# mLSTM attention and a squared-ReLU FFN on one core: from chunk 10 on, an even chunk's attention goes directly behind the FFN1 section, and FFN2 runs unbroken

## The chip, the cores and the metric

The kernel runs on one core of one Trainium2 chip. Times are device microseconds of that core. The engines are named as in the profile: PE (TensorE matmuls), PEld (its weight loads), DVE (VectorE), ACT (ScalarE), POOL (GpSimd), SP (SyncE, which here only issues DMAs). L405 means line 405 of the kernel.

## What is computed

Four batches of eight heads with 768 tokens and a head size of 40 go through an mLSTM cell; its output, reshaped to 3072 rows of 320, goes through an FFN with a squared ReLU and 2048 hidden columns. Inputs and output are float32.

```python
# attention, for each token t (C, n and m are the running state of a head)
m_new = maximum(f[t] + m, i[t])
f_stab, i_stab = exp(f[t] + m - m_new), exp(i[t] - m_new)
C = f_stab * C + i_stab * outer(v[t], k[t])
n = f_stab * n + i_stab * k[t]
y[t] = sigmoid(o[t]) * (C @ q[t]) / maximum(abs(n @ q[t]), 1.0)
# FFN on x = y, reshaped to (3072, 320)
h = maximum(x @ w_in, 0)
out = (h * h) @ w_out
```

## The kernel before

**Chunks.** The attention is done in 24 chunks of 128 tokens, six to a batch. Chunk s is computed in chunk form: scores of keys against queries (`scores`, L565), a weight for each pair from the gates (`weigh`, L498: eight exponentials on ACT, then `vw` on POOL), their product (`weighted`, two operations on DVE, L608), and `attend_begin` and `attend_end` (L774, L835), which multiply these with the values, add the part of the carried state C, and make the next state. The first chunk of a batch (0, 6, 12, 18) has no part of C (L799); the last makes no new state.

**FFN.** Two chunks make a group of 256 rows. FFN1 of a group is done in two halves, each `ffn1_open` (four accumulators X, Y, V, Z in four PSUM banks), then `ffn1_close`, and `ffn1_rows` (L1165), 64 records in which 64x64 pieces of the array are used for the last 64 rows of w_in. The closing ends in one ACT operation and four DVE adds (L1181 to L1185). FFN2 is `ffn2_fast`, four steps of 32 PE records (L1056). Both are a Strassen-like scheme with seven products, so each step is followed by adds, and sums of operands (`sums`, L1051) are made on DVE. Full-array matmuls (FFN1's main part, FFN2) and 64-row ones (scores, attention, rows) alternate on PE.

**The order.** Everything is issued in an order written out by hand, and each engine works in that order. From chunk 6 on, the loop at L1426 goes through parts n, four to a section: section s = 6 + n // 4, and `at` = n % 4. An even section is FFN2 of a group, an odd one FFN1 of a group two further; the last sections, from 24 on, have no attention. In each section of chunk s stand:

- even s, at 0: `scores(s)`, the transpose of the next chunk's keys and queries (`turn_kq`, L403 to L405, DVE), `weighted(s)`, then FFN2's first step, then `ffn1_square` for the second half of the FFN1 section before it (four ACT operations)
- even s, at 1: `attend_begin(s)`, `scores(s + 1)`, `attend_end(s)`, then the second FFN2 step
- odd s, at 1 (between FFN1's first opening and closing): `attend_begin(s)`, `ffn1_rows`, `attend_end(s)`; behind the closing `turn_kq(s + 1)`
- at 1 also, behind `attend_end`: `decays(s + 1)` (ACT, L496), `mask(s + 1)` (POOL, L478), `decay_C(s + 1)` (POOL, Cd), loads of later chunks (POOL's DMAs), and on SP `store_num` (L868, the transposed result tn to DRAM), `load_num` (L873, four DMAs), `load_squares(s + 2)` (L398, four DMAs: keys and queries of chunk s + 2 into one of the two kqT buffers), and in even sections `load_A(s + 2)` (L429, two DMAs)
- at 2: FFN's third step or second opening; then `weigh(s + 1)`, in even sections `weighted(s + 1)`, `normalise_turned(s)` (ten DVE operations, L885 to L898), `store_rows` and `load_rows` (SP); in odd sections `load_A(s + 2)`; `scale_q(s + 1)` (DVE, L761)
- at 3: FFN's last step or second closing, and DMA issues of POOL for later chunks

**The write that separates the two halves of attention.** The last thing of `attend_begin` is a one-element DVE operation. It reads an element that the half's last matmuls write, and writes into a spare column of the keys, which the first weight load of `attend_end` reads:

```python
# L787, L790
end, spare = out[1][DP : DP + 1, 2 * P + D1 : 2 * P + D1 + 1], d["kq"][DP : DP + 1, 0, 2, DP - 1 :]
nc.vector.tensor_scalar(spare, end, scalar1=0.0, scalar2=None, op0=ALU.mult)
```

So PE enters `attend_end` only when DVE has come to this operation in its own order.

**PSUM.** In this loop three banks (`at`) hold the attention's two outputs and some scores, and five (`h_ps`) are used in turn by FFN1, FFN2 and the scores that ask for "h".

Of the kernel before, what the change touches and what calls it, by code (L numbers as in the profile page):

```python
# [29 lines left out]
def kernel(  # L30
# [372 lines left out]
    def turn_kq(s):  # L403
        t = kqT_b[s % NKT][:].rearrange("p n j t -> p (n j t)")
        nc.vector.transpose(t, t)  # L405
# [159 lines left out]
    def scores(s, o=(False, False)):  # L565
        d = st[s]

        sc = [bank(o[i]) for i in range(2)]
        d["sc"] = sc
        if s >= KQ_SQ:  # L570
            if s >= ROT:
                d["sc"] = [t.rearrange("p j t -> p (j t)")[:, : 3 * P].rearrange("p (e t) -> p e t", e=2) for t in sc]
            for e in range(2):
                for late_keys in range(2):
                    for c in range(2):
                        for i in range(2):
                            rows = slice(DP * i, DP * i + D)
                            start = e == late_keys == 0
                            if s < ROT:
                                j, keys = 2 * late_keys + e, HALVES[c]  # L580
                                to, t0 = sc[i][HALVES[c], j, :], 0
                            else:
                                j, keys = 2 * (c ^ late_keys) + e, HALVES[late_keys]
                                to = d["sc"][i][HALVES[c], e, slice(0, DP) if late_keys else slice(DP, 3 * DP)]
                                t0 = DP * late_keys
                            nc.tensor.matmul(  # L586
                                to, lhsT=d["kT"][rows, j, keys], rhs=d["qT"][rows, j, t0:], start=start, stop=True,
                                skip_group_check=True,
                            )
            return  # L590
        for j in range(PR):
            for i in range(2):
                rows = slice(DP * i, DP * i + D)
                nc.tensor.matmul(  # L594
                    sc[i][:, j, :], lhsT=d["kT"][rows, j, :], rhs=d["qT"][rows, j, :], start=True, stop=True,
                )
# [556 lines left out]
    def ffn1_rows(g, q, first):  # L1153
        xT, xs = st["xT", g], st["xs"]
        X, Y, V, Z = st["f1"]
        lo, hi = HALVES
        pairs = (
            ((X, lo, xT[lo, 0, 2, :], False), (Y, hi, xT[hi, 1, 2, :], first)),
            ((V, lo, xT[lo, 1, 2, :], first), (Z, hi, xs[hi, 1, :], False)),
        )  # L1160
        for pair in pairs:
            for n in range(4):
                for cols in HALVES:
                    for to, rows, rhs, start in pair:
                        nc.tensor.matmul(  # L1165
                            to[cols, n, :], lhsT=w_in2[rows, 4 * q + n, cols], rhs=rhs,
                            start=(start and n == 0), stop=True, skip_group_check=True,
                        )
# [34 lines left out]
    def do(f, s):  # L1203
        if 0 <= s < NT:
            f(s)
# [97 lines left out]
    for u in range(8):  # L1303
        s = 2 + u // 2
# [114 lines left out]
    for g in range(NG):  # L1419
        parts += [(2, g, i) for i in range(4)]  # L1420
        if g + 2 < NG:
            parts += [(1, g + 2, i) for i in range(4)]
    ROUNDED = (17, 18)
    assert ROUNDED[-1] == len(pieces)

    for n, (which, g, i) in enumerate(parts):  # L1426
        s, at = NB + n // 4, n % 4
        if n == len(ROUNDED):
            brought.close()
            late = ctx.enter_context(tc.tile_pool(name="late", bufs=1, side="right"))  # L1430
        even = s % 2 == 0
        fast = which == 1
        if n == 2:
            half_tanh(6)
            half_tanh(7)
        if at == 0 and even:
            do(scores, s)
            if n > 0:
                do(turn_kq, s + 1)
            do(weighted, s)  # L1440
        if n == 0:
            turn_kq(7)
            pair_up(8)
            load_rows(4)
            rounding.words()
            rounding.join()
        if at == 1:
            do(attend_begin, s)
            if n == 5:
                sums_of_weights(3)  # L1450
            if even:
                do(lambda s: scores(s, ("h", "h")), s + 1)
            if fast:
                ffn1_rows(g, 0, True)
            do(attend_end, s)
            do(decays, s + 1)
            do(mask, s + 1)
            if not even and not fast:
                do(turn_kq, s + 1)
            do(decay_C, s + 1)  # L1460
            if not fast and not even:
                do(turn_squares, s - 1)
            if even and s > NB:
                do(load, s + 3)
            do(store_num, s)
            if n == 1:
                normalise_turned(5)
                store_rows(5)
                turn_squares(4)
            if n == 5:  # L1470
                load_rows(6)
            do(load_num, s)
            if n == 1:
                load_rows(5)
                weigh(7, masked=True)
                sums_of_win(2)
            do(load_squares, s + 2)
            if even:
                do(load_A, s + 2)
        if n == 3:  # L1480
            load_o(8)
            load_o(9)
            sums_of_weights(0)
        if n == 8:
            sums(1, slice(0, NPAIR), (3,))
        if n == 9:
            sums(1, slice(0, NPAIR), (4,))
            sums_of_weights(2)
            turn_squares(6)
        if which == 2 and i == 3 and g == NG - 2:  # L1490
            sums(g + 1, slice(0, NPAIR), (2,))
        if which == 2 and g > 1 and i < 2:
            sums(g, slice(0, NPAIR), (3 + i,))
        if at == 3 and even and NB < s and s // 2 - 1 < NG:
            sums_of_x(s // 2 - 1)
        if at == 2 and not fast:
            if even and n > 2:
                do(turn_squares, s - 1)
            do(scale_q, s + 1)
        if at == 3:  # L1500
            if s % 4 == 3:
                for r in range(s + 1, min(s + 5, NT) if n > 7 else 10):
                    half_tanh(r)
        if n == 10:
            half_tanh(10)
            half_tanh(11)
        if fast:
            if i % 2:
                if n == 7:
                    sums(1, slice(0, NPAIR), (2,))  # L1510
                ffn1_close(g, i // 2, i == 1)
                if at == 1:
                    do(turn_kq, s + 1)
                    if n > 5:
                        do(turn_squares, s - 1)
            else:
                ffn1_open(g, i // 2)
                if i == 0 and g > 2:
                    sums(g - 1, slice(0, NPAIR), (2,))
            if at == 2:  # L1520
                do(scale_q, s + 1)
            if n == 6:
                sums(1, slice(0, NPAIR), (1,))
        elif g == 0:
            ffn2(i)
        else:
            ffn2_fast(g, i)
        if at == 2:
            if n > 2:
                do(lambda s: weigh(s, masked=True), s + 1)  # L1530
            ffn1_square()
            if even:
                do(weighted, s + 1)
            do(normalise_turned, s)
            do(store_rows, s)
            if n == 2:
                pair_up(9)
                turn_squares(5)
                sums_of_x(2)
                load(8)  # L1540
            if not even:
                do(load_A, s + 2)
            if n > 2:
                do(load_o, s + 5)
                do(load_rows, s)
            if s == NB + 1:
                pair_up(s + 3)
        if n in (5, 6):
            load(4 + n)
            load_o(5 + n)  # L1550
        if even and at == 3 and s > NB:
            do(pair_up, s + 3)
            do(pair_up, s + 4)
        if even and at == 3 and s > NB:
            do(load, s + 4)
        if n == 4:
            sums_of_weights(1)
        if n == 3:
            turn_halves()
        if n in (12, 25):  # L1560
            spread_slots(2 + n // 25)
        if at == 0:
            ffn1_square()
        if n < len(ROUNDED):
            while rounding.done < ROUNDED[n]:
                rounding.step()
# [30 lines left out]
```

## Time and profile before

| what | us |
|---|---|
| median of three runs | 487.77 |
| the three runs | 487.77, 488.3, 483.75 |
| span of the profiled execution | 484.7 |
| PE busy in it | 476.5 |
| DVE busy in it | 342.4 |
| one FFN2 section from chunk 10 on, first score matmul to next FFN1 | 18.3 to 19.3 |

The profile gives its span, from the first to the last instruction, and no separate time for that execution; one of the three runs is 1.0 below this span and two are 3.0 and 3.6 above it, so what lies around the span can't be told from the scatter between executions. A line of a timeline gives the start in us, the time taken, the engine, the line of the kernel, the operation with its output and inputs, the tile and the number of merged records; a bracket behind it gives the idle time of the engine and what ended it. Matmuls overlap, so starts, not durations, are what costs are read from.

### The profile page before, as it was taken

Reading aid. Unit: us, or ns where it says so; the run is one execution under the profiler, and the core shown is the slowest. Engines: PE = TensorE matmul, PEld = TensorE weight load, DVE = VectorE, ACT = ScalarE, POOL = GpSimd, SP = SyncE. Lnnn points to the kernel's source line nnn. Section 1 sums busy time; section 2 is a strip of 40 time slices with the busy share of each in tenths; the row PEclk is TensorE's granted clock in tenths of the full one; section 3 lists DMA queues with packets and bytes.
Section 4 is the critical chain, followed back from the end, with each engine's and each line's share of the span. In section 5 each row is a group of like instructions: output and inputs, shape, how many; then the busy total and the mean of one; then the engine's idle time right before and its main releaser. Section 6 shows DMA issues by size and latency. Waiting matters only on the chain.

```text
span 484.7 us, 15567 instructions
## 1 busy us (share of the span) xinstructions
PE 476.5 (98%) x6307; PEld 443.9 (92%) x6309; DVE 342.4 (71%) x722; ACT 243.2 (50%) x534; POOL 224.9 (46%) x336
## 2 busy tenths in 40 slices
PE   8999999999999999999999999999999999999997
PEld 4886787779999999999999999999999999999997
DVE  7979868798897866767775956857966956635441
ACT  4699799634743723923622931742942741513300
POOL 5464544656598096098097088089083040020000
PEclk9999999999999999999999999999999999999999
DMA  8999998788977776777677758849655612200000
GB/s 174 200 261 248 284 210 207 213 151 201 183 148 197 141 149 177 135 151 178 129 132 197 139 98 223 142 98 225 126 110 143 126 46 84 57 28 3 1 27 28
DMA packets 192696, 69.93 MB, mean 144 GB/s; under 512 B 158128, under 2 KB 181360, under 8 KB 192624
## 3 DMA queue, kind: packets, MB, share of 16 engines
q1 hardware_dynamic: 186400, 58.68, 56.0%
q0 software_dynamic: 6080, 10.16, 8.6%
q8 instruction: 50, 0.82, 0.7%
q14 instruction: 22, 0.18, 0.1%
q10 hardware_dynamic: 144, 0.10, 0.1%
HBM read 55.69 MB, written 18.92 MB: 154 GB/s over the span
## 4 chain that ended last, share of the span: by engine, by line
PE 83%; DMA 5%; DVE 4%; ACT 3%; SPq 2%; issue 1%; POOL 1%; DVEq 0%; POOLq 0%; ACTq 0%
PE h_ps L1056 32%; PE h_ps L1132 24%; PE h_ps L1165 7%; PE h_ps L972 4%; PE h_ps L1010 4%; PE numT L819 3%; PE numT L799 2%; ACT g_c L515 1%; PE numT L830 1%; DMA num_rows<-tn 1%; DMA kqT<-kq_rows 1%; PE h_ps L983 1%; PE tp L594 1%; PE h_ps L586 1%; PE tp L586 1%
## 5 line engine op out<-in xcount | busy, mean ns | idle before, releaser
L478 POOL TENSOR_SCALAR_AFFINE_SELECT A_bc<-A_bc 64x512 f32<-64x512 f32 x32 | 23.1, 721 | 88.1 <-ACT kq L496 59.3
L1146 ACT COPY r_sb<-h_ps 128x512 f32<-128x512 f32 x20 | 11.7, 585 | 84.6 <-PE h_ps L1132 84.6
L1056 PE MATMUL h_ps<-T,S 128*128 128x160 f32 x352 | 51.7, 300 | 0.0
L1056 PEld LDWEIGHTS h_ps<-T,S 128*128 128x128 f32 x352 | 48.9, 190 | 0.4 <-ACT g L1181 0.2
L1056 PE MATMUL h_ps<-w_out,g 128*128 128x160 f32 x336 | 49.2, 303 | 0.0
L1056 PEld LDWEIGHTS h_ps<-w_out,g 128*128 128x128 f32 x336 | 46.1, 190 | 1.3 <-issue 0.9
L1072 DVE TENSOR_TENSOR y_sb<-y_sb,h_ps 128x160 f32<-128x160 f32 x44 | 14.0, 318 | 45.2 <-PE h_ps L1056 45.0
L1132 PE MATMUL h_ps<-xT,w_in 128*128 128x128 f32 x320 | 43.4, 278 | 0.7 <-issue 0.7
L1132 PE MATMUL h_ps<-lent_t,w_in 128*128 128x128 f32 x320 | 42.3, 275 | 0.0
L1132 PEld LDWEIGHTS h_ps<-xT,w_in 128*128 128x128 f32 x320 | 39.2, 192 | 1.6 <-issue 1.2
L1132 PEld LDWEIGHTS h_ps<-lent_t,w_in 128*128 128x128 f32 x320 | 38.9, 192 | 0.8 <-issue 0.8
L375 POOL DMA_DIRECT2D va<-in_v_dram x64 | 39.3, 626 | 0.0
L1165 PE MATMUL h_ps<-xT,w_in 64*64 64x128 f32 x960 | 39.2, 272 | 0.0
L1132 PE MATMUL h_ps<-lent_t 128*128 128x128 f32 x320 | 39.1, 275 | 0.0
L1132 PEld LDWEIGHTS h_ps<-lent_t 128*128 128x128 f32 x320 | 37.3, 192 | 0.2 <-issue 0.2
L509 ACT ACTIVATE A_bc<-A_bc,b_R 128x64 f32<-128x64 f32 (+1 forms) x128 | 35.7, 361 | 1.0 <-POOL A_bc L478 0.6
L1165 PEld LDWEIGHTS h_ps<-xT,w_in 64*64 64x64 f32 x960 | 34.8, 133 | 1.3
L853 DVE STREAM_TRANSPOSE tn<-numT 128x256 f32<-128x256 f32 x36 | 14.0, 428 | 27.9 <-PE numT L799 18.9
L1124 POOL TENSOR_TENSOR lent_t<-xT 128x128 f32<-128x128 f32 (+1 forms) x18 | 15.6, 887 | 32.7 <-DVE xT L938 32.7
L972 PE MATMUL h_ps<-xT,w_in 128*128 128x256 f32 x128 | 30.1, 386 | 0.5 <-POOL w_in L236 0.4
L1056 PE MATMUL h_ps<-w_out,g_c 128*128 128x160 f32 x192 | 28.0, 302 | 0.0
L972 PEld LDWEIGHTS h_ps<-xT,w_in 128*128 128x128 f32 x128 | 23.4, 190 | 5.0 <-POOL w_in L236 1.3
(233 smaller groups left out, 1148.1 us busy)
## 6 DMA issues: line engine op xcount, KB each, us to landing
A_bc<-a_slots SPq DMA_DIRECT2D x32, 256.0 KB, 4.3
kq<-num_rows SPq DMA_DIRECT2D x80, 64.0 KB, 2.2
num_rows<-tn SPq DMA_DIRECT2D x18, 256.0 KB, 2.5
raw<-in_moe_w_out_dram SPq DMA_DIRECT2D x7, 640.0 KB, 5.7
kqT<-kq_rows SPq DMA_DIRECT2D x34, 128.0 KB, 3.8
og<-in_o_gate_dram SPq DMA_DIRECT2D x24, 160.0 KB, 4.9
x_rows<-x_sb SPq DMA_DIRECT2D x20, 192.0 KB, 3.4
xT<-x_rows SPq DMA_DIRECT2D x80, 48.0 KB, 3.3
```

The source lines that it names most:

```text
L375: eng.dma_start(dst[HALVES[n], PR * (1 - late_keys) : PR * (2 - late_keys)], src[HALVES[late_keys], PR * m : PR * (m + 1)],)
L478: nc.gpsimd.affine_select(part, part, compare_op=ALU.is_ge, fill=-1e30, base=0, pattern=[[0, PR], [0, 2], [1, DP]], channel_multiplier=-1,)
L509: nc.scalar.activation(A[0][:, x, to], A[0][:, x, to], AF.Exp, bias=b_R[:, b, c, own, x : x + 1],)
L819: nc.tensor.matmul(d["numT"][m][HALVES[e], i, t0:], lhsT=va_w[s % NKQ][keys, at * D1 : at * D1 + DP], rhs=rhs, start=(s % NB == 0 and i == ...
L853: nc.vector.transpose(to[:, 2 * m : 2 * m + 2], d["numT"][m].rearrange("p c t -> p (c t)"))
L972: nc.tensor.matmul(hs[i][:, n, :], lhsT=w_in[:, a, fb * P : (fb + 1) * P], rhs=xT[:, :, a, :], start=(n == 0 and a == 0), stop=False,)
L1010: nc.tensor.matmul(st["o_ps"][j], lhsT=st["g2", 0][:, fb, j * P : (j + 1) * P], rhs=w_out[:, fb, :], start=(fb == 0), stop=(fb == NF - 1),)
L1056: nc.tensor.matmul(to, lhsT=lhsT[:, p], rhs=rhs[:, p, :], start=(start and p == 0), stop=(p == NPAIR - 1), skip_group_check=True,)
L1072: add = lambda to, a, b: nc.vector.tensor_tensor(to, a, b, op=ALU.add)
L1124: sub = lambda to, a, b: eng.tensor_tensor(to, a, b, op=ALU.subtract)
L1132: nc.tensor.matmul(to[:, n, :], lhsT=lhsT[:, 4 * q + n, :], rhs=rhs, start=(start and n == 0), stop=True, skip_group_check=True,)
L1165: nc.tensor.matmul(to[cols, n, :], lhsT=w_in2[rows, 4 * q + n, cols], rhs=rhs, start=(start and n == 0), stop=True, skip_group_check=True,)
```

## The change

From section 10 on (`EARLY = 10`), an even chunk's whole block of "at 1" (attend_begin, scores of the next chunk, attend_end, decays, mask, stores and loads) is issued at 0, ahead of FFN2's first step, so it follows the 64-row matmuls that end the FFN1 section. The even chunk's own scores move into the odd section before, between `ffn1_rows` and `attend_end`; its `weigh` and `weighted` then stand in that section ahead of the second opening (`weigh` stood behind it, `weighted` in the even section). The scores of both kinds now take one bank of the three and one of the five. `turn_kq` moves one section earlier in the order: it is issued at 3 of section s for chunk s + 2, ahead of that part's closing or last FFN2 step.

```diff
+    EARLY = 10
...
-        if at == 0 and even:
+        if at == 0 and even and s < EARLY:
             do(scores, s)
             if n > 0:
                 do(turn_kq, s + 1)
...
-        if at == 1:
+        if at == (0 if even and s >= EARLY else 1):
             do(attend_begin, s)
             if n == 5:
                 sums_of_weights(3)
             if even:
-                do(lambda s: scores(s, ("h", "h")), s + 1)
+                do(lambda s: scores(s, ("h" if s < EARLY else False, "h")), s + 1)
             if fast:
                 ffn1_rows(g, 0, True)
+                if s + 1 >= EARLY:
+                    do(lambda s: scores(s, (False, "h")), s + 1)
             do(attend_end, s)
...
         if at == 3:
+            if s + 2 >= EARLY and even or s + 1 >= EARLY and not even:
+                do(turn_kq, s + 2)
...
                 if at == 1:
-                    do(turn_kq, s + 1)
+                    if s + 1 < EARLY:
+                        do(turn_kq, s + 1)
                     if n > 5:
                         do(turn_squares, s - 1)
             else:
+                if at == 2 and s + 1 >= EARLY:
+                    do(lambda s: weigh(s, masked=True), s + 1)
+                    do(weighted, s + 1)
                 ffn1_open(g, i // 2)
...
         if at == 2:
-            if n > 2:
+            if n > 2 and (even or s + 1 < EARLY):
                 do(lambda s: weigh(s, masked=True), s + 1)
```

## The prediction

> **What bounds the kernel now.** First the head of the page: which engine is full, and at what clock.
>
> ```profile
> span 484.7 us, 15567 instructions
> PE 476.5 (98%) x6307; PEld 443.9 (92%) x6309; DVE 342.4 (71%) x722; ACT 243.2 (50%) x534; POOL 224.9 (46%) x336
> ...
> PEclk9999999999999999999999999999999999999999
> ```
>
> TensorE is busy for 98% at the full clock, so time comes off only by fewer or cheaper PE records, and whatever makes PE wait is paid in full. Second, the timeline of PE over one even section (chunk 20; gaps between these starts are the costs used below), and over the one FFN2 section that has no attention in it.
>
> ```profile
> 345.55 0.85 PE L586 MATMUL tp<-kqT 40*64 40x128 f32 x32
> 346.32 2.44 PE L1056 MATMUL h_ps<-w_out,g 128*128 128x160 f32 x16
> ...
> 351.05 0.45 PE L799 MATMUL numT<-kq,C 40*64 40x128 f32 x8
> ...
> 351.96 0.88 PE L586 MATMUL h_ps<-kqT 40*64 40x128 f32 x32
> 352.66 0.40 PE L830 MATMUL numT<-vw,kq 64*64 64x41 f32 x16
> ...
> 353.46 1.76 PE L1056 MATMUL h_ps<-w_out,g 128*128 128x160 f32 x11
> ```
>
> ```profile
> 418.92 2.44 PE L1056 MATMUL h_ps<-w_out,g 128*128 128x160 f32 x16
> ...
> 434.24 1.05 PE L1132 MATMUL h_ps<-xT,w_in 128*128 128x128 f32 x8
> ```
>
> Third, the chain of waits around chunk 14, one of the few places where PE does wait: a kqT load ends it through VectorE (DVE) alone.
>
> ```profile
> 233.81 2.87 DMA kqT<-kq_rows
> ...
> 238.26 1.16 DVE kqT L405
> 239.42 0.53 DVE A_bc L608 x2
> ...
> 241.72 0.17 DVE kq L790
> 241.89 0.04 issue
> 241.93 0.44 PE numT L830 x16
> ```
>
> L790 is the one-element write into kq that closes attend_begin; attend_end's first weights read that element, so PE can't enter attend_end before DVE, in its order, has come to it. Fourth, what stands before it: DVE and SP behind an FFN1 section (chunk 19, then 20).
>
> ```profile
> 344.94 0.69 DVE L1182 TENSOR_TENSOR r_sb<-r_sb,h_ps 128x512 f32<-128x512 f32 x1
> 345.55 0.68 DVE L1183 TENSOR_TENSOR g_c<-r_sb,h_ps 128x512 f32<-128x512 f32 x1
> 346.15 0.68 DVE L1184 TENSOR_TENSOR g_c<-r_sb,h_ps 128x512 f32<-128x512 f32 x1
> 346.75 0.68 DVE L1185 TENSOR_TENSOR g_c<-r_sb,h_ps 128x512 f32<-128x512 f32 x1
> 347.34 1.24 DVE L405 STREAM_TRANSPOSE kqT<-kqT 128x1024 f32<-128x1024 f32 x1
> ```
>
> ```profile
> 336.28 0.38 SPq L868 DMA_DIRECT2D num_rows<-tn  x1
> 339.52 1.75 SPq L873 DMA_DIRECT2D kq<-num_rows  x4
> 341.38 2.52 SPq L398 DMA_DIRECT2D kqT<-kq_rows  x4
> ```
>
> FFN2's first quarter (4.7 us) hides all of this today: attention starts only at 351.05.
>
> **The change, part by part.**
>
> *PE, the gain.* An even section, first score matmul to the next FFN1, lasts 18.70, 18.32, 19.25, 18.89, 18.26, 18.89 and 18.70 us for chunks 10 to 22. Afterwards it is attention (351.05 to 353.46: 2.41; chunks 12 and 18 begin a batch and lack L799: 314.54 to 316.50, 1.96) and unbroken FFN2 (434.24 - 418.92 = 15.32): 17.73, or 17.28. That saves 0.97 + 1.04 + 1.52 + 1.16 + 0.98 + 1.16 + 0.97 = 7.8 us; the 1.52 holds the wait of chunk 14. The scores come back in seven odd sections at 352.66 - 351.96 = 0.70: 4.9. Net -2.9 us, for one change of matmul shape less per pair.
>
> *The cover that goes, the loss.* Behind FFN1's last row matmuls PE now needs 0.09 to begin, then 1.61 us to reach attend_end (351.05 to 352.66; 1.39 without L799). DVE's order there becomes: transpose of kqT for the next odd chunk (moved ahead of the closing adds), four adds, L790. From the landing of that kqT: 0.05 to wake (the DVE wait that ends at 233.89 starts its work at 233.94), 1.16 transpose, 4 x 0.60 adds (starts 344.94 to 347.34), 0.16 for L790, 0.06 to PE: 3.83 us. The same transpose gates the scores that stand between the two halves, but earlier, so L790 decides.
>
> When does kqT land? Taken from the end of DVE's queued waits at L405, or last issue plus landing (2.6 to 5.0 us; 3.5 taken for chunk 17), against the old first score matmul, where FFN1's rows end: odd chunk 9: 163.2 against 161.80; 11: 199.5 against 198.11; 13: 236.7 against 234.50; 15: 273.1 against 272.72; 17: 309.9 against 309.21; 19: 346.26 against 345.55; 21: 383.1 against 382.50. Late by 1.4, 1.4, 2.2, 0.4, 0.7, 0.7, 0.6. PE comes 0.70 later (scores in the odd section). The load comes later by what its chain is: attention's end, tn, SP's store, four loads of num, four of kqT (tn's end 335.53 to landing 346.26, 10.7 us). Where SP was busy anyway when tn was ready (1.6, 0.03, 0.8, 0.4, 0.7, 0.75, 0.55 us), the 0.70 is absorbed up to that: shifts 0, 0.7, 0, 0.3, 0, 0, 0.15. Wait = lateness + shift + 3.83 - 0.70 - 1.61 (1.39 for evens 12 and 18): for 11 to 21: 3.8, 3.7, 2.2, 2.4, 2.2, 2.3.
>
> For chunk 9 DVE itself is later than the load. Weigh now precedes the opening copy, weighted the opening adds: POOL's mask ends at 155.95, eight exponentials (2.24) 158.2, vw (0.74) 159.05, weighted, two adds, scale and normalise (1.0 + 1.4 + 0.6 + 1.9) 163.95; then 3.78 to PE, which would be there at 164.1: 3.6 us. Sum of waits 3.6 + 16.6 = 20.2 us.
>
> *The rest.* The same reorder in other odd sections costs up to 1 us where POOL's DMA issues delay the mask (PE's second accumulation waits for the opening add); that moves PE and not the load, so it is contained in the waits above: 0 more, and it counts by itself only if those waits vanish. The even section's transpose (1.16) now precedes FFN2's last add, which frees the bank of the next opening's fourth block. Free 1.35 to 2.05 us after the opening in most pairs (2.64 before chunk 13), needed at 2.68: 0 to 1.1 us, taken as 0, since PE's shift loosens POOL there. ScalarE: four decays (1.45) move ahead of the m1 copy; the A load they need lands some 5 us after the rows end, the copy is needed at about 9: hidden, up to 1 us per pair if not. SP: store, four num loads, four kqT loads and two A loads of even chunks leave one FFN2 quarter earlier, as do POOL's mask, Cd and seven k/v loads; their users are a section away: 0, between -1 and +1 per pair. PSUM: fourteen bank turns per pair as before: 0.
>
> [...] PEclk stays at 9 with no PE idle time above about 1 us in this stretch. [...]
>
> *Sum.* 484.7 - 2.9 + 20.2 = 502.0 us on the profiled execution. The median of the runs is 487.77, 3.1 above its span, and the runs scatter from 483.75 to 488.3. Carried to the median: 505.1.
>
> **Rivals.**
>
> A, the forecast: 505 us.
>
> B, kqT is not late: DVE takes its transpose in front of the row matmuls' end. For: SP's chain might shorten, as three loads land in 2.7 us. Against: it is anchored to the odd attention's end, and seven of seven landed after the rows. It decides if kqT lands over 2 us earlier. Then only the adds remain: chunk 17's first add starts 1.20 after the rows begin, L790 reaches PE at 3.82, PE is there after 1.71 + 0.09 + 1.61 = 3.41: 0.4 per pair, 0.6 in two: 3.2 - 2.9: 488.1, no slower.
>
> C, the change does what it says and L790 never holds PE: 487.77 - 2.9 = 484.9, 0.6% faster. It needs L790 another 0.4 to 0.6 us sooner than B's four adds let it come, and they wait for the row matmuls themselves; no row speaks for it.
>
> D, half: loads land about 1.2 us earlier as the longer sections loosen DMA and SP: 7 x 1.2 less: 497.
>
> E, more: landings at 5.0 instead of 2.9 us, or the reordered exponentials, the fourth bank and the A load each showing: 1 to 1.5 us per pair more, 513 to 516.
>
> **How the numbers follow.** A 0.60, D 0.16, E 0.12, B 0.09, C 0.03. The range runs from 494 (D with a little less lateness) to 513. About 1% is what a measurement of this kernel tells from no change; B and C give within 1%, with a little for scatter across the line: faster 0.02, same 0.10, slower 0.88.
>
> **What would show it.** Right: in each even section from chunk 10, PE stands between L586 and attend_end, released by L790, 1.5 to 2 us, and before L586 up to 2 us, released by L405; in the chain of waits kqT loads, L405, L1182 to L1185 and L790 once per pair; FFN2 in one piece of 15.3 us; PE's share near 95%. Wrong: L405 starting before the rows end, or an even section near 17.7 us. A shorter chain from tn to landing, or an order on DVE other than the program's, would make the forecast too high.

## The result, and the profile after

The changed kernel takes **513.5 us** (median of 6 runs, 508.62 to 514.37); the kernel before, run beside it, takes 488.09 us (median of 6, 483.75 to 488.46). The ratio is 1.0506, with a 95% interval of 1.0472 to 1.054: 25.4 us slower. The forecast was 505.1, 17.3 us slower, with a range up to 513.0; the median lies 0.5 us above its end (1.0506 x 487.77, the median of before that the forecast started from, is 512.5). The profiled execution has a span of 512.5 us. A run with a profile shows both its time and its span: 514.22 against 512.5 here, 1.7 us around it. The kernel before shows the same distance in its later runs (486.35 against 484.6, for one), so its profiled execution of 484.7 took about 486.4, somewhat less than its median. Of the 3.1 us that the forecast put between span and median, about 1.7 lie around the span, and the rest is scatter between executions.

The page of the changed kernel, its head:

```profile
span 512.5 us, 15507 instructions
...
PE 486.2 (95%) x6309; PEld 453.1 (88%) x6309; DVE 340.1 (66%) x722; ACT 243.8 (48%) x534; POOL 226.9 (44%) x336
...
PEclk9999999999999999899899999889989999999999
```

PE's share fell from 98% to 95%, so PE waits more. But its busy time rose by 9.7 us, from 476.5 to 486.2, though the change saves PE work: the 8s in the clock row, absent before, are slices in which the granted clock was below full (0.983 in the mean of the execution, 1.000 before). So there are two losses here. First the waits of PE (engine, line, what it waited for: us in total, times, longest):

```profile
PE numT L830 <- DVE kq L790: 10.7, 7, 1.6
PE tp L586 <- DVE kqT L405: 4.2, 6, 1.0
...
PE h_ps L1132 <- DVE r_sb L1148: 0.9, 1, 0.9
```

The two waits that were forecast stand there, once per pair, seven times behind L790 and six behind L405. The chain of waits around chunk 12 shows what they are made of (start, us, what); the same pieces come back once per pair for chunks 10 to 22:

```profile
201.61 3.11 DMA kqT<-kq_rows
...
205.15 1.26 DVE kqT L405
...
208.16 0.60 DVE g L1185
...
208.79 0.17 DVE kq L790
...
209.00 0.44 PE numT L830 x16
```

The kqT load ends, DVE transposes, adds four times, comes to L790, and only then does PE enter `attend_end`. From the transpose's start at 205.15 to L790's at 208.79 it is 3.64 us, what the forecast had (1.16 + 4 x 0.60 = 3.56, beside its wake). FFN2 follows in one piece, as the diff says. PE's timeline over the same stretch:

```profile
206.45 0.32 PE L586 MATMUL tp<-kqT 40*64 40x128 f32 x1 [0.86 <-DVE kqT L405]
...
209.00 0.44 PE L830 MATMUL numT<-vw,kq 64*64 64x41 f32 x16 [1.56 <-DVE kq L790]
...
209.62 4.12 PE L1056 MATMUL h_ps<-w_out,g 128*128 128x160 f32 x16
...
226.62 1.05 PE L1132 MATMUL h_ps<-xT,w_in 128*128 128x128 f32 x8
```

The brackets give the idle time; by starts, as the prediction counts, a wait is somewhat longer (207.22, the last score matmul, to 209.00, less a usual 0.04: 1.74). The second loss is in the third line: the first sixteen FFN2 matmuls take 4.12 us where the same group took 2.44 before, and the section lasts 226.62 - 209.62 = 17.00 us, where 15.32 was forecast. The busy times in two windows around that place (window, length, busy time and records of PE, PEld, DVE, ACT, POOL, then the granted clock):

```profile
206.45:209.86 3.41, 1.85 (x65) 1.65 (x66) 2.58 (x6) 1.30 (x4) 0.66 (x1) 1.00 0.84 140
209.86:213.27 3.41, 3.41 (x14) 3.41 (x14) 2.07 (x5) 0.14 (x1) 2.99 (x4) 0.50 0.25 86
```

Behind a stretch of 3.41 us in which PE was busy for 1.85, the clock is 0.50 for the next 3.41. It happens in four of the seven pairs (from 209.86, 250.82, 373.7, and for twice as long from 329.32): FFN2 takes 16.99, 16.99, 17.90 and 16.99 us there instead of 15.32, 7.6 us in all.

The pairs from chunk 9 on (start of one FFN1 section to that of the next) took 36.8, 35.9, 37.3, 37.9, 35.9, 37.0, 36.8 us and take 40.3, 40.1, 40.7, 39.8, 41.6, 41.2, 39.0: 25.2 more in all. From the starts: waits 18.3, half clock 7.6, scores that take 0.78 instead of 0.66 in the even section 0.7, a longer break between the instructions at chunk 15 0.65, less the saving of 2.9 as forecast: 24.4. The other 0.8 are not accounted for. The 2.5 us by which this execution is already behind at the start of section 9 (146.20 against 143.73) lie ahead of all that the change touches.

### The profile page after: what moved, and what is told of

The parts are those of the page before. It is cut to its first block, busy times and chain, and to the rows that moved or that the text cites. A ratio compares the mean times of both kernels' runs of the same rounds, so it can differ in the third digit from the quotient of the medians.

```text
span 512.5 us, 15507 instructions
## 1 busy us (share of the span) xinstructions
PE 486.2 (95%) x6309; PEld 453.1 (88%) x6309; DVE 340.1 (66%) x722; ACT 243.8 (48%) x534; POOL 226.9 (44%) x336
## 4 chain that ended last, share of the span: by engine, by line
PE 61%; DMA 14%; DVE 10%; SPq 8%; issue 3%; ACT 2%; POOL 0%; DVEq 0%; POOLq 0%; ACTq 0%
PE h_ps L1056 33%; PE h_ps L1132 11%; DMA kqT<-kq_rows 4%; PE h_ps L1165 4%; DMA num_rows<-tn 4%; SPq L398 4%; SPq L873 3%; DMA raw<-in_moe_w_out_dram 3%; PE h_ps L972 2%; DVE kqT L405 2%; PE numT L819 2%; PE numT L799 1%; DMA x_rows<-x_sb 1%; PE tp L586 1%; PE numT L830 1%
## 5 line engine op out<-in xcount | busy, mean ns | idle before, releaser
L1056 PE MATMUL h_ps<-w_out,g 128*128 128x160 f32 x336 | 55.8, 329 | 0.0
L1056 PEld LDWEIGHTS h_ps<-w_out,g 128*128 128x128 f32 x336 | 52.9, 212 | 1.1 <-issue 0.9
L1056 PEld LDWEIGHTS h_ps<-T,S 128*128 128x128 f32 x352 | 50.0, 193 | 0.0
L1132 PEld LDWEIGHTS h_ps<-xT,w_in 128*128 128x128 f32 x320 | 39.2, 192 | 1.8 <-issue 1.2
L1132 PEld LDWEIGHTS h_ps<-lent_t 128*128 128x128 f32 x320 | 37.3, 192 | 0.2 <-issue 0.2
L496 ACT ACTIVATE kq<-A_bc 64x256 f32<-64x256 f32 x56 | 20.1, 406 | 30.9 <-DMA A_bc<-a_slots 30.7
L1124 POOL TENSOR_TENSOR lent_t<-xT 128x128 f32<-128x128 f32 (+1 forms) x18 | 12.9, 738 | 41.1 <-DVE xT L938 36.9
L1181 ACT ACTIVATE g<-h_ps 128x512 f32<-128x512 f32 x12 | 7.1, 594 | 47.2 <-PE h_ps L1132 38.7
```

The lines of the kernel that those rows point to most:

```text
L496: nc.scalar.activation(e[rows, j : j + 2, :], A[rows, i::2, own * P : (own + 1) * P], AF.Exp)
L1056: nc.tensor.matmul(to, lhsT=lhsT[:, p], rhs=rhs[:, p, :], start=(start and p == 0), stop=(p == NPAIR - 1), skip_group_check=True,)
L1132: nc.tensor.matmul(to[:, n, :], lhsT=lhsT[:, 4 * q + n, :], rhs=rhs, start=(start and n == 0), stop=True, skip_group_check=True,)
```

## Experiments

The theory: DVE's queue (transpose of the late kqT, four adds, L790), standing open on PE's path, costs about 17 of the 25 us (12.0 on L790 and 5.3 on L405 by starts), and the clock that drops behind it the rest. The first rival: the load alone is too late. The second: the 64-row matmuls or the order of `weigh` cost it in themselves. Diffs are against the changed kernel, unless another is named. Medians of different experiments were taken beside different runs of the kernel before, which has medians of 486.35 to 488.09 there, so a difference between two of them is good to about 2 us; the ratios allow for that.

**1. The odd chunk's transpose behind the four adds.** The sum of the work ahead of PE stays, its order changes.

```diff
-            if s + 2 >= EARLY and even or s + 1 >= EARLY and not even:
+            if s + 2 >= EARLY and even:
                 do(turn_kq, s + 2)
...
                 ffn1_close(g, i // 2, i == 1)
+                if at == 3 and s + 1 >= EARLY:
+                    do(turn_kq, s + 2)
```

> The odd section's kqT transpose goes behind the closing's four adds instead of ahead of them; nothing else differs from the changed kernel (513.5 us). Theory (DVE's queue in front of L790 sets the wait): the sum of waits is what four adds and a transpose take, wherever the transpose stands. The scores then wait longer (the adds end about 3.6 us after the row matmuls begin, the transpose 1.2 us later: about 2.2 us of wait before L586 in every pair), and the 1.6 to 1.8 us before attend_end shrink to about 0.1, because L790 now stands directly behind the transpose that the scores wait for. About 0.45 us per pair less in six pairs and 0.7 more where the load was early (chunk 16): 511 us, if the clock does as now. Rival (attend_end waits for PE's own drain or for PSUM, not for DVE): the wait before attend_end stays at 1.75 us and comes on top of the longer wait before the scores: 520 us or more. Second rival (only the late load matters, the adds are hidden): waits before the scores as now, 0.9 us, none before attend_end: about 500 us.

514.94 us, ratio 1.058 (1.0552 to 1.0608). The waits:

```profile
PE tp L586 <- DVE kqT L405: 14.9, 7, 2.4
```

All of it now stands ahead of the scores, none before L790: the sum is that of the two waits before (10.7 + 4.2 = 14.9). It is DVE's queue, wherever PE meets it. The time is 4 us above the number expected, and the mean granted clock is 0.980 in its span of 513.4 us, which is six windows of 3.41 us at half clock (513.4 x 0.020 x 2 = 20.5 us); the changed kernel's five make 0.983.

**2. The four adds behind L790.** DVE issues them after `attend_begin`'s last write instead of in the closing.

```diff
+        def adds():
+            tt(U2[:], U2[:], Y[:], op=ALU.add)
+            ...
+        if later:
+            st["adds"] = adds
...
             do(attend_begin, s)
+            if "adds" in st:
+                st.pop("adds")()
```

> The four adds of the closing that stands in front of an even chunk's attention are issued behind L790; the transpose stays ahead of both. Theory: L790 now needs only the transpose and PE, so the wait before attend_end (6 x 1.74 + 1.55 = 12.0 us in the changed kernel) goes to under 0.1 us a pair, the wait before the scores stays (0 to 1.2 us a pair, 5.3 us in all), and the four windows or more of half clock, which I take to come from the two waits together, go too (about 7.7 us): 513.5 - 12 - 7.7 = 494 us; 501 us if the clock still drops. Rival (PE's drain or PSUM): no change, 513 us.

492.61 us, ratio 1.0124 (1.0097 to 1.015): 20.9 us less than the whole change (18.6 by the two ratios; the seven pairs together take 262.1 us where they took 282.7, 20.6 less). DVE's timeline for the same chunk 12 (the first add follows at 204.89):

```profile
203.32 1.25 DVE L405 STREAM_TRANSPOSE kqT<-kqT 128x1024 f32<-128x1024 f32 x1 [0.70 <-DMA kqT<-kq_rows]
204.71 0.16 DVE L790 TENSOR_SCALAR kq<-numT 1x1 f32<-1x1 f32 x1
```

L790 comes 1.39 us after the transpose's start instead of 3.64. No wait on L790 is left, 1.9 us on L405, and the clock is 1.0 throughout. The four adds in front of L790 are the bulk of the loss, the half clock behind the wait (7.6 us) included. The wait on L405, which the expectation left as it was, fell too, from 4.2 us.

**3. The kqT load earlier.** SP issues the four loads of kqT ahead of the four loads of num.

```diff
+            if s + 1 >= EARLY:
+                do(load_squares, s + 2)
...
-            do(load_squares, s + 2)
+            if s + 1 < EARLY:
+                do(load_squares, s + 2)
```

> SP issues the four kqT loads directly behind the store of num, in the 2.4 to 4 us in which it otherwise waits for that store to land, instead of behind the four loads of num. Theory: kqT lands some 4.7 us earlier, so DVE comes to the transpose at the end of normalise, about 0.9 us before the rows end; no wait before the scores, and the wait before attend_end falls to about 1.2 us a pair: 5.3 us and about 4 us less, 504 us, and less by up to 7.7 if the clock stays up: 497 to 504. Rival (the load's lateness is all of the loss): no wait at all, 485 to 488 us. Rival (DVE's queue is full anyway and the load is not what it waits for): no change, 513 us.

510.69 us, ratio 1.0494 (1.0462 to 1.0526): the 497 to 504 us expected are missed. SP's loads of num, behind those of kqT (issued from 195.23 on), and DVE in chunks 11 and 12 show why:

```profile
199.03 2.25 SPq L873 DMA_DIRECT2D kq<-num_rows  x4
```

```profile
202.93 0.17 DVE L885 TENSOR_SCALAR dm<-kq 128x8 f32<-128x8 f32 x1 [1.71 <-DMA kq<-num_rows]
...
205.20 1.25 DVE L405 STREAM_TRANSPOSE kqT<-kqT 128x1024 f32<-128x1024 f32 x1 [0.34 <-issue]
```

kqT now lands before DVE wants it, but num's loads are pushed behind it, and the ten operations of normalise that use num stand ahead of the transpose on DVE. They waited until 202.93, and the transpose starts at 205.20, where it had started at 205.15. Two loads on one queue feed two operations on another, so bringing one forward brought little: PE's waits on L405 fell from 4.2 to 2.8 us and those on L790 stayed (10.3), and the two ratios, 1.0506 and 1.0494, can't be told apart. The late load is one of two chains that hold the transpose about equally long.

**4. Experiments 2 and 3 together.** The diff is that of both.

> Both edits: adds behind L790, and kqT loads between the store and the loads of num. Theory: neither wait is left (under 0.2 us a pair), the clock is at full speed throughout, and the saving on PE that the forecast worked out (2.9 us) shows, less about 1 us in the section of chunk 9 where weigh stands ahead of the opening's copy: 486 us, against 488 before. If something else in the new order costs time (A loads, the bank of the fourth block, ScalarE's order), it is what is left over 486.

493.35 us, ratio 1.013 (1.0105 to 1.0155); the 486 expected are missed. Left over are small waits: 1.6 us on L405 (the scores of three chunks), 1.0 us of FFN2 on an ACT operation (L1076), and

```profile
PE h_ps L1132 <- DVE r_sb L1148: 0.9, 1, 0.9
PE h_ps L1132 <- ACT r_sb L1146: 0.8, 1, 0.8
```

These two are section 9's: FFN1's second accumulation waits for the opening's copy and add, which now stand behind `weigh` and `weighted`. The prediction put this at nothing as long as the larger waits stood, and in experiment 2 and here they no longer stand. The waits listed come to 4.3 us, of some 7 that are missing to the 486 expected; the rest was not taken apart.

**5. Weigh and weighted put back behind the second opening,** on top of experiment 4.

```diff
-                if at == 2 and s + 1 >= EARLY:
-                    do(lambda s: weigh(s, masked=True), s + 1)
-                    do(weighted, s + 1)
                 ffn1_open(g, i // 2)
...
-            if n > 2 and (even or s + 1 < EARLY):
+            if n > 2:
                 do(lambda s: weigh(s, masked=True), s + 1)
...
-            if even:
+            if even or s + 1 >= EARLY:
                 do(weighted, s + 1)
```

> Adds behind L790, kqT loads between store and loads of num, and weigh and weighted of even chunks back behind the second opening. Theory: in the section of chunk 9 the openings' copy and adds no longer stand behind the exponentials, which took 1.0 + 1.1 us of PE there: 2 us less than with both edits alone (493.4): 491.5 us. Rival (these waits only move to weighted, which DVE then reaches after normalise): no difference.

494.71 us, ratio 1.016 (1.0122 to 1.0197), no gain. The waits of section 9 are gone, but L405's grew from 1.6 to 3.6 us, by one of 1.9 in chunk 10, and FFN2 waits for ACT's L1181 (1.7 us). DVE in section 9 shows where the 1.9 comes from:

```profile
163.27 0.17 DVE L885 TENSOR_SCALAR dm<-kq 128x8 f32<-128x8 f32 x1 [1.95 <-DMA kq<-num_rows]
```

Num's load ends DVE's idle time, normalise follows, and the transpose starts only at 165.19, when PE, no longer held up in section 9, already waits. The execution's mean granted clock is 0.997, where experiment 2 has 1.000; over 492.2 us that is about one window of 3.41 us at half clock (492.2 x 0.003 x 2 = 3.0 us). The wait moved.

**6. PE kept busy in the wait.** Between scores and `attend_end`, 28 matmuls of zeros in bf16 into unused columns of a score bank; they compute nothing that is used. If the half clock comes from PE's empty time, this takes it away without touching DVE's queue.

```diff
+    def fill(s):
+        t = st[s]["sc0"][:, 3, :]
+        for _ in range(28):
+            nc.tensor.matmul(t, lhsT=zeros[...], rhs=zeros[...], start=True, stop=True, ...)
...
                 do(lambda s: scores(s, ("h" if s < EARLY else False, "h")), s + 1)
+                if s >= EARLY and s + 1 < NT:
+                    fill(s + 1)
```

> The changed kernel with 28 dummy bf16 matmuls of 128 columns (zeros, into unused columns of a score bank) between the scores and attend_end of every even section from chunk 10: some 1.6 us of PE work, which fits into the 1.6 to 1.8 us that PE waits there for L790. They compute nothing that is used. Theory: the wait itself isn't shortened, but PE isn't idle in it, so the windows of half clock that the changed kernel has (five of 3.41 us, FFN2 sections of 16.99 and 17.90 instead of 15.32 us, 7.6 us in all) go: 513.5 - 7.6 = 506 us, clock 1.0. Rival (half clock comes from something else, or from the wait before the scores alone, or zeros don't count as work): clock 0.98 as now, 513 to 515 us.

505.42 us, ratio 1.0402 (1.0353 to 1.0451): 8.1 us less than the changed kernel by the medians, about 5 by the two ratios, and 7.7 by the seven pairs of the profiled executions (275.0 against 282.7), by adding work. The clock row, and the same place in chunk 12:

```profile
PEclk9999999999999999999999999999999999999999
```

```profile
205.56 1.82 PE L1221 MATMUL tp<-zeros 128*128 128x128 bf16 x28
...
207.94 2.44 PE L1056 MATMUL h_ps<-w_out,g 128*128 128x160 f32 x16
```

The zeros fill the wait (0.2 us is left on L790), the granted clock is 1.000 in the mean, PE is busy for 3.27 of the 3.50 us from 204.40 on, the first FFN2 group takes 2.44 us again, and every FFN2 section from chunk 10 on 15.32. So the clock term is the 7.6 us by which these sections were too long, and it went when PE's empty time was filled. The forecast, which had no clock term, was 505.1.

**7. Attention back behind FFN2's first step,** the rest of the change kept.

```diff
-        if at == (0 if even and s >= EARLY else 1):
+        if at == 1:
```

> All of the changed kernel but its first point: the even chunks' attention goes back behind FFN2's first quarter; scores of even chunks stay in the odd section, the transposes, weigh and weighted stay where the change put them. Theory (the cover of FFN2's first quarter hid DVE's queue): no wait before the scores, none before attend_end, clock 1.0; one shape change per pair is not saved but the scores of the even chunk cost 0.70 instead of 0.78 us: 487 us, about 1 to 2 us of it in the section of chunk 9, where weigh stands ahead of the copy: within 1% of before. Rival (the earlier transposes, or the weigh and weighted ahead of the second opening, carry the loss): 495 us or more.

495.99 us, ratio 1.02 (1.0153 to 1.0248); 487 was expected, so the cover does not give everything back: some 8 us of loss lie in what the change moves besides. Its longest wait:

```profile
PE h_ps L1132 <- DVE r_sb L1148: 3.1, 4, 0.9
```

It is the order of `weigh` again, in four sections here; 1.9 us are left on L790. Three runs took the rest apart.

**8. Experiment 7 with weigh and weighted put back as in 5.**

> The even chunks' attention behind FFN2's first quarter, and weigh and weighted of even chunks behind the second opening as before: what is left of the change is where the even chunk's scores stand and that the transposes come earlier. Theory: with attention back alone (496.0 us) the loss sat in four odd sections in which the copy and adds of the second opening stood behind the exponentials (PE waits of 1.2 + 3.1 us, and half a microsecond around each); with these back too they go: 489 to 490 us, and the one wait of 1.7 us on L790 at chunk 16 may stay. Rival (the earlier transposes carry the loss): no less than 494 us.

497.2 us, ratio 1.018 (1.0136 to 1.0225): no gain. The waits on L1148 are gone, but in the profiled execution (500.57 us, the longest of six) 2.6 us stand on L790 and 1.9 on L1181 in their place, so putting `weigh` back doesn't remove the remaining loss.

**9. Only the even chunks' scores moved, with their transposes and `weighted`, which must come ahead of them or go with them;** against the kernel before, and the odd transposes where they were.

```diff
-        if at == 0 and even:
+        if at == 0 and even and s < EARLY:
             do(scores, s)
...
+        if at == 0 and even and s >= EARLY:
+            do(turn_kq, s + 1)
...
+                if s + 1 >= EARLY:
+                    do(lambda s: scores(s, (False, "h")), s + 1)
```

> The kernel before with one part of the change: from chunk 10 the even chunks' scores stand in the odd section ahead, with weighted there too, behind the second opening; their transpose is early as it must be, but the odd chunks' transposes stand where they stood before, in the even section behind the closing's adds, and attention stands behind FFN2's first quarter. Theory now: of the 9 to 10 us that stayed when attention was put back (497.2 us), the larger part is the odd chunks' transpose, which waits for its load ahead of the four adds: 489 to 490 us without it. Rival (the moved scores and weighted, with their PSUM banks, carry it): 494 us or more.

487.75 us against 487.33, ratio 1.0027 (1.0001 to 1.0054). The scores' new place costs 0.4 us by the medians and 2.6 at most by the interval. This kernel differs from experiment 8's in one thing, where the odd chunks' transposes stand, and that is worth 9.5 us (497.2 against 487.75).

**10. Only the odd chunks' transpose moved,** against the kernel before: ahead of the second closing's adds.

```diff
-            if n > 0:
+            if 0 < n and s < 10:
                 do(turn_kq, s + 1)
...
+            if not even and s > 8:
+                do(turn_kq, s + 2)
```

> The kernel before with one part of the change alone: from chunk 11 the odd chunks' transpose is issued in the odd section ahead of the second closing's adds, where it waits for its kqT load, instead of behind them. Everything else as before, so FFN2's first quarter covers DVE. Theory: DVE then ends its work ahead of L790 about a microsecond later, near the time that PE comes to attend_end: 0 to 0.8 us a pair, 488 to 493 us, with any wait before attend_end released by L790 and none before the scores. Rival (without the cover being gone, the order on DVE costs nothing): 487 us.

497.47 us, ratio 1.0206 (1.0167 to 1.0246); both numbers expected were too low. One line of the diff, harmless by the look of it, costs 10 us. The clock isn't the bulk of it: the one run with a granted clock of 1.0 took 495.18, 7.9 more than the kernel before. The profiled execution took 503.29 us, 5.8 more than the median, so its profile is read for its order of events and not for its sum. Its longest wait (L819 has another 3.5 us on the same L608), and its chain around chunk 20:

```profile
PE numT L799 <- DVE A_bc L608: 5.2, 3, 2.7
```

```profile
321.84 2.92 DMA kqT<-kq_rows
...
325.23 1.25 DVE kqT L405
...
328.84 0.48 DVE A_bc L608
...
329.36 0.91 PE numT L819 x16
```

Here too kqT's late load holds DVE's queue; the adds and then `weighted` (L608) stand behind it, and attention, although behind FFN2's first step, waits for `weighted`. Followed back, the chain goes on through SP's queue, where the store of num (3.43 us, from 313.84) and before it that of normalise's rows (5.09 us, from 305.66) stand ahead of the kqT loads.

**11. All mends of one kind together:** experiment 5, the odd transpose ahead of `weighted` and normalise, the decays behind the copy.

```diff
+            if not even and s + 1 >= EARLY:
+                do(turn_kq, s + 2)
...
-            do(decays, s + 1)
-            do(mask, s + 1)
+            if at == 1:
+                do(decays, s + 1)
+                do(mask, s + 1)
...
+            if at == 0 and even and s >= EARLY:
+                do(decays, s + 1)
+                do(mask, s + 1)
+                do(decay_C, s + 1)
```

> The former, and two more: in odd sections the kqT transpose stands ahead of weighted and normalise (which waits for num's load) instead of behind them, and in even sections the four decays stand behind the copy of FFN2's first product instead of ahead of it. Theory: the last waits before the scores (0.4 to 1.0 us in three pairs) and before FFN2's second quarter (0.5 and 1.0 us in two) go, and what remains is the saving of 2.9 us on PE: 485 us beside 487 to 488 of before, ratio 0.994. Rival: DVE is still full behind an FFN1 section, and L790, which now comes behind normalise, is what PE waits for: 490 us or more.

497.15 us, ratio 1.0194 (1.0148 to 1.024); 485 was expected. Its longest wait:

```profile
PE h_ps L586 <- ACT g L1181: 3.8, 2, 2.0
```

With the third of its kind (1.9 us) that is 5.7 us in chunks 12, 16 and 20, and 2.2 us stand on L790, which now comes behind normalise. A score bank now comes free only when ACT has done L1181, and there ACT first does the sigmoids of four chunks, which had been hidden by FFN2.

**12. The best that these runs point to:** experiment 4 from chunk 12 on, the transpose ahead of normalise and the decays behind the copy as in 11, the sigmoids behind L1181.

```diff
-    EARLY = 10
+    EARLY = 12
...
-            if s % 4 == 3:
+            if s % 4 == 3 and s + 1 < EARLY:
...
+                if at == 3 and s % 4 == 3 and s + 1 >= EARLY:
+                    for r in range(s + 1, min(s + 5, NT)):
+                        half_tanh(r)
```

> Both edits (adds behind L790, kqT loads between store and loads of num), and four more: the new order starts at chunk 12, so the section of chunk 9, where POOL's mask is latest, keeps the old one; in odd sections the kqT transpose stands ahead of normalise, weigh and weighted staying where the change put them; in even sections the four decays stand behind the copy of FFN2's first product; and the sigmoids of the output gate stand behind the closing's ACT operation instead of ahead of it. Theory: each wait that both edits alone left has its work moved from in front of it, so six pairs save 0.3 to 0.5 us each: 485.5 us beside 487, ratio 0.995 to 1.0. Rival: the engines behind an FFN1 section are too full for any order (DVE has some 9 us of work between two openings there), waits of 1 us turn up elsewhere: 489 us or more.

488.11 us (12 runs) against 487.25 (17 runs), ratio 1.0016 (0.999 to 1.0041): no difference that can be measured. The waits from chunk 9 on are almost gone (0.4 us on L790 and 0.9 on L1148), and the last three pairs take 35.62, 36.42 and 36.42 us where they took 35.87, 36.96 and 36.77: 0.25 to 0.54 each, about the saving that the prediction had worked out as 2.9 / 7 = 0.4; the two pairs ahead of them save 0.2 each. The first pair of the new order loses 1.3 us, 0.9 of it at L1148, so of 1.6 us saved 0.3 is left in this profile, too little for the runs to show. Attention stands directly behind the row matmuls here too, so these 64-row matmuls in themselves cost nothing that shows in the ratio of 1.0016.

## Why the prediction was right, and where it was not

*PE's saving, 2.9 us.* Held in kind, and about in size. FFN2 in one piece lasts 15.32 us wherever the clock is full and it doesn't wait, and with next to nothing in the way (the last five pairs of experiment 12) a pair is 0.2 to 0.54 us shorter, 0.3 in the mean where 0.4 was forecast. The sum over seven pairs was not measured by itself.

*The waits, 20.2 us.* The mechanism and place are shown: L405, four adds and L790 once per pair, 3.64 us from transpose to L790, experiment 1 moves it by moving the transpose alone, and experiment 2 removes its larger part by moving the adds alone. The size is 18.3 by starts. Each L790 wait is 1.74 (1.55 in chunk 16) and does not depend on the load, since PE's scores wait for the same transpose; it is the transpose-to-L790 time less PE's own way there. Only the part ahead of the scores varies with the lateness, 0 to 1.2 us where the prediction gave up to 2. That the sum came so near is in part luck: for even chunks 12 to 22, forecasts of 3.8, 3.7, 2.2, 2.4, 2.2 and 2.3 met 2.8, 2.5, 1.55, 2.9, 2.9 and 2.4, and the misses, from -1.2 to +0.7, largely cancel. For the chunk 9 and 10 pair, 3.6 was forecast and 0.54 + 1.74 + 1.0 = 3.3 came, but not by the reason given. The forecast had DVE later than the load there; in the trace DVE is through with normalise, and its transpose waits 0.69 us for the load (it starts at 166.46), and the 1.0 is PE's wait on L1148 in section 9, which the prediction had counted as contained in the others.

*When kqT lands.* Late in nearly every pair, as forecast. What the step left out is that normalise, which needs num, stands ahead of the transpose on DVE: a second chain of about the same length (experiment 3). It made no difference to the forecast; it is why an earlier load, as in rival D, doesn't help by itself.

*"The rest".* The order of weigh was put at 0 more, counting by itself only if the waits vanish: that is what experiments 4 and 7 show. Not seen by this step is that the odd transpose's place costs 10 us even with FFN2's first step as cover (experiment 10). The cover was read as belonging to L790 alone; in that experiment `weighted` stands in the same queue behind the same adds. In the full change the account from the starts leaves no room for it beside L790's wait: both stand behind the same late transpose.

*The clock.* This is the step that failed: the forecast's sum has no term for it. Measured were 7.6 us by FFN2's sections, and 7.7 less in the pairs of experiment 6, which takes the half clock away. The page of before has PEclk at 9 throughout, and the longest wait of PE from chunk 9 on is 0.7 us there. In the changed kernel no single wait exceeds 1.6 us, and the clock drops all the same: what the drops go with is all of PE's empty time within one 3.41-us window (the last section has the windows). PE was busy for 39 or 54% of the window ahead of each drop. The drops lie on one grid (250.82 - 209.86 = 12 x 3.413, 329.32 - 250.82 = 23 x 3.413).

*The rivals.* B (488.1) and C (484.9) fell: kqT is late and L790 holds PE. D (497) would have needed loads 1.2 us earlier, and experiment 3, in which the load did come ahead of DVE's need, stayed at 510.69. E's number (513 to 516; its 1 to 1.5 us per pair add up to 512 to 516) is met, but not by its reasons: the last load takes 2.75 to 3.11 us to land and not 5.0, the fourth bank and the A load do not show, and the reordered exponentials do in one section of seven, for 1.0 us. The forecast's 502.0 of span plus 7.6 for the clock would have been 509.6, against 512.5 measured, of which 2.5 lie ahead of section 9; the waits came 1.9 us under the forecast and small terms of 0.7, 0.65 and 0.8 over it.

What stays open: why three of the seven pairs keep the full clock with nearly the same wait is put down to where that grid falls (PE is busy for 56 to 60% of the window there, for 39 to 54% ahead of the drops); that is the author's estimate from one trace, and no run was made for it. What is left of the loss in experiments 4 and 7 was only taken apart in part.

## What to carry to other kernels

Before work is moved up against an engine's wait, list everything that stands in the other engine's queue ahead of the instruction that releases it; a one-element write used as a barrier cost the whole queue in front of it here, 10.7 us of PE's waits in seven pairs. Put adds that nobody waits for behind such a write: that alone gave back 20.9 of 25.4 us here, the half clock included. Price a row of small gaps on TensorE together with the half clock that can follow them (7.6 us here), before a saving of 0.4 us per pair is taken.

## What the runs showed of the hardware

In the changed kernel the half clock came without a long idle gap: the longest wait of PE was 1.6 us. Windows of 3.41 us in which PE was busy for 39, 54, 54 and 54% were followed by one (that at 39% by two) at clock 0.50, and windows at 56, 58, 58 and 60% were not. Two of them in the form used above, the second with its successor:

```profile
325.91:329.32 3.41, 1.33 (x55) 1.08 (x44) 3.39 (x5) 0.00 (x0) 0.00 (x0) 1.00 0.82 223
...
411.24:414.65 3.41, 1.90 (x48) 1.73 (x49) 2.36 (x8) 1.44 (x4) 0.92 (x2) 1.00 0.72 137
414.65:418.06 3.41, 3.41 (x28) 3.41 (x27) 1.48 (x2) 1.97 (x4) 1.72 (x2) 1.00 0.28 97
```

These are windows of one execution, and the ends of matmuls are modelled in them, so no limit is read from the step between 54 and 56%. In experiment 6, 1.82 us of useless matmuls in the wait of chunk 12, and as many in the others, went with a granted clock of 1.000 and made the seven pairs 7.7 us faster.
